# A one-core attention + MLP kernel: a new written-out order of tasks, with the first q and k ahead of w_tok and the casting loads behind the selector and masks

## The chip, the cores and the metric

The kernel runs on one core of a Trainium2 chip. The metric is the device time of one execution in microseconds (us), the median of three runs. The engines are named as the profile names them: PE (TensorE), DVE (VectorE), ACT (ScalarE), POOL (GpSimd) and SP (SyncE, which here only starts transfers). ACT and POOL start transfers too.

## What is computed

Four batches (B = 4) of 768 tokens, 8 heads of 64, so 512 channels. First attention with a window of 128 tokens and 4 sink tokens, then a residual MLP that mixes tokens and channels:

```python
scores = scale * np.matmul(q, k.transpose(0, 1, 3, 2))
keep = is_sink | in_window            # rel in [0, 128), or one of the first 4 keys
a = softmax(where(keep, scores, -1e9))
x = matmul(a, v)                      # heads side by side: (4, 768, 512)

a1  = alpha1 * x + beta1
tok = np.einsum('ts,bsd->btd', w_tok, a1)          # w_tok is 768 x 768
u   = x + lam * tok
a2  = alpha2 * u + beta2
ch  = np.maximum(a2 @ w_ch1, 0.0) @ w_ch2          # 512 -> 2048 -> 512
out = u + lam * ch
```

All inputs and the output are float32 in memory; the matmuls take float16 operands and sum in float32.

## The kernel before

**Stages.** The work is cut per batch. For batch 0: load q, k and v, cast to float16, transpose q and k on PE (`trans`, lines 482 to 535), scores S = k q (`scores`, `scores_by_pair`), exp on ACT, mask, P V (`pv`, lines 707 to 785) with the sums of the softmax from a column of ones, normalisation on DVE (lines 748 and 749). Then `tok` (lines 845 to 873): 36 matmuls of 128x128 by 128x512 with the transposed w_tok, then the transposes of u (`uTp`), `mlp1` (lines 926 to 947: 512 channels to 2048, ReLU), and `mlp2` (for batch 0) or seven products in Strassen's manner (`prod`, for batches 1 to 3). While batch b is in its MLP, the attention of batch b+1 is laid between its matmuls. The start, up to the first `tok` matmul of batch 0, has no earlier batch to be laid beside.

**Tiles.** A q or k tile holds two heads ("hp", a pair, 0 to 3) of all 768 tokens; t = 0 is q, t = 1 is k. For batch 0 the pair 0 is loaded by SP as float32 (`nat0_0_0`, `nat0_0_1`, line 402) and cast on DVE (line 157). The pairs 1 to 3 are loaded by POOL's queue, which casts in flight (`CASTING`, line 322, and line 395); these six transfers are called the casting loads here. v comes in twelve pieces of 128 KB (`load_v0`, line 429), w_tok in six rows of 384 KB (`load_wtok`, line 440), each then cast (`cast_wtok`, lines 819 or 821) and transposed on PE (line 814). w_ch1 comes in four casting transfers of POOL's queue, w1[0] to w1[3] (`load_w1`, line 453), which `mlp1` needs by quarters of its 16 columns fi: fi 0 to 3 need w1[0], 4 to 7 w1[1], 8 to 11 w1[2], 12 to 15 w1[3].

**The selector, masks and identity** are made on POOL: `make_iden` (lines 330 and 331), `make_masks` (five instructions, lines 338 to 348), `make_bm` (the block mask, lines 359 and 363), `make_sel` (lines 370 and 374). `make_bias` (line 353, DVE) turns the masks into a bias that PE adds to the scores.

**The order is written out by hand.** Every step is a task, registered by `add` with a running number. `emit` (lines 54 to 74) walks a table `ORDER` of task numbers and issues each task on the engine that `ENGINES` gives to it by its number (0 ACT, 1 DVE, 2 PE, 3 POOL, 4 SP). Each engine then takes its own instructions strictly in that order. `HOMES` gives every buffer its place: two buffers of one kind and one home share memory, so the later one waits for the readers of the earlier. `IDLES` lists matmuls on zeros ahead of a task, as (task, home of the PSUM bank, how many): they fill PE's waiting time (line 148).

Fixed costs, due times and dependencies in the `add` calls served a planner; at run time only the order, the engines, the homes and the data decide.

**Tasks that the change and the prediction speak of** (number: what, line, engine in the kernel before):

- 6 and 7: loads of q and k of pair 0 (402, SP); 26: first row of w_tok (440, SP); 9, 8, 15, 12, 14, 13: casting loads of k1, q1, k3, q2, q3, k2 (395, POOL)
- 45 and 48: casts of q0 and k0 (157, DVE); 46 and 49: their transposes (512, PE); 47 and 50: copies of these from PSUM (155, ACT)
- 51 and 52: transposes of q1 (509, PE) and their copy (157, DVE); 61 and 62: the same for k3
- 90, 91: scores of pair 0, first key block, and its exp (686, 691); 109, 110: scores of key block 4 for four heads, and their exp (622, 644)
- 63, 64, 65, 66: casts of v pieces; 72 to 89: the six rows of w_tok (cast, transpose, copy); 81 and 82: cast and transpose of row block 3, ahead of `tok`
- 39: product of alpha1 and lam (1169); 43 and 44: transpose of alpha2 and beta2 and its copy
- 115, 118, 121, 124, 127, 130: halves of the float16 input of `tok` (758, POOL); 32 to 35: w1[0] to w1[3]
- 213: the first `tok` matmuls; 295: the first `mlp1` column that needs w1[3]
- 179, 178, 197: the loads `wst_w2_0`, `lam_b` and `wst_w2_12` (449 and 1240, SP); 36: a small transfer on SP that waits for w1[1], and holds back all that stands behind it on SP
- 653, 660: scores of batch 2, key blocks 0 and 1 (622); 656 and 654: the two exps of block 0 (644)

Of the kernel before, what the change touches and what calls it, by code (L numbers as in the profile page):

```python
# [77 lines left out]
def kernel(  # L78
# [119 lines left out]
    for r in range(NR):  # L198
# [18 lines left out]
        26, 6, 9, 7, 10, 5, 11, 8, 18, 15, 72, 19, 1, 12, 3, 0, 4, 2, 22, 14, 73, 74, 45,  # L217
        48, 46, 17, 39, 49, 47, 53, 13, 40, 50, 41, 90, 95, 43, 91, 51, 54, 103, 52, 16, 44,
        61, 104, 42, 96, 109, 100, 62, 107, 110, 63, 55, 28, 108, 92, 56, 101, 21, 68, 65,
        59, 93, 20, 69, 97, 102, 111, 94, 24, 98, 57, 60, 30, 112, 105, 23, 58, 99, 113,  # L220
        128, 106, 114, 116, 25, 131, 135, 78, 115, 64, 27, 138, 31, 32, 117, 132, 29, 129,
        136, 33, 122, 66, 125, 34, 123, 137, 119, 139, 126, 35, 79, 70, 120, 140, 124, 84,
        71, 80, 133, 130, 141, 67, 146, 85, 134, 121, 147, 144, 75, 118, 158, 86, 154, 148,
        159, 145, 142, 87, 149, 150, 155, 160, 143, 76, 88, 151, 156, 81, 77, 166, 152, 162,
        167, 89, 127, 82, 163, 213, 83, 168, 209, 164, 165, 214, 210, 153, 217, 179, 211,
        178, 157, 197, 229, 36, 212, 215, 218, 185, 216, 226, 230, 219, 176, 161, 177, 220,
        169, 223, 222, 232, 225, 224, 221, 227, 237, 233, 279, 238, 234, 228, 273, 280, 182,
        171, 204, 257, 274, 175, 277, 258, 200, 231, 259, 278, 246, 260, 295, 199, 384, 241,
        248, 188, 186, 291, 296, 247, 172, 243, 289, 174, 181, 242, 293, 292, 187, 170, 290,
        267, 37, 294, 271, 358, 268, 198, 285, 349, 272, 381, 301, 286, 366, 351, 303, 302,  # L230
        189, 297, 378, 173, 304, 281, 180, 352, 203, 249, 190, 282, 298, 379, 250, 287, 380,
        192, 353, 385, 288, 206, 283, 386, 369, 375, 367, 265, 284, 368, 202, 370, 266, 363,
        376, 371, 253, 377, 201, 299, 254, 372, 364, 183, 382, 191, 300, 373, 615, 365, 275,
        374, 383, 357, 261, 276, 408, 262, 387, 263, 184, 409, 205, 195, 239, 411, 264, 410,
        395, 269, 396, 240, 397, 270, 196, 388, 614, 621, 235, 412, 400, 194, 244, 398, 236,
        401, 255, 617, 251, 245, 256, 389, 390, 399, 252, 311, 359, 207, 193, 391, 424, 616,
        335, 425, 393, 341, 426, 392, 336, 648, 427, 634, 413, 394, 312, 636, 414, 428, 419,
        404, 420, 415, 360, 405, 313, 429, 208, 422, 337, 416, 361, 441, 421, 622, 402, 314,
        423, 442, 626, 403, 305, 638, 315, 406, 430, 640, 316, 435, 431, 306, 641, 355, 436,
        443, 619, 437, 338, 649, 618, 438, 362, 317, 432, 637, 407, 307, 433, 345, 444, 339,  # L240
        439, 635, 318, 445, 450, 434, 639, 644, 319, 451, 628, 452, 620, 440, 308, 645, 340,
        453, 417, 446, 323, 447, 418, 320, 309, 448, 324, 321, 658, 322, 329, 449, 642, 659,
        454, 325, 625, 643, 330, 646, 347, 455, 326, 623, 343, 647, 464, 344, 456, 465, 348,
        466, 460, 457, 467, 650, 327, 458, 331, 461, 629, 459, 472, 462, 632, 463, 653, 356,
        651, 656, 627, 332, 38, 654, 480, 333, 342, 624, 652, 473, 310, 476, 468, 471, 470,
        469, 481, 474, 488, 885, 477, 475, 482, 492, 655, 490, 493, 350, 483, 478, 514, 491,
        516, 489, 657, 479, 515, 660, 517, 630, 882, 665, 518, 663, 354, 328, 666, 502, 880,
        661, 664, 498, 879, 519, 508, 499, 346, 503, 678, 662, 512, 509, 679, 504, 513, 487,
        484, 671, 485, 676, 486, 506, 677, 877, 548, 505, 672, 680, 507, 526, 549, 546, 527,
        631, 334, 522, 674, 681, 528, 547, 907, 523, 534, 903, 529, 633, 682, 675, 878, 542,  # L250
        683, 535, 890, 689, 543, 550, 685, 684, 690, 510, 551, 494, 511, 673, 667, 544, 495,
        668, 891, 496, 686, 545, 901, 687, 669, 497, 693, 888, 688, 883, 530, 694, 670, 700,
        531, 524, 897, 701, 698, 500, 691, 525, 696, 699, 552, 501, 697, 704, 553, 558, 695,
        705, 904, 692, 562, 559, 706, 909, 887, 707, 563, 564, 898, 708, 702, 566, 565, 910,
        715, 703, 567, 532, 716, 889, 713, 533, 709, 714, 896, 520, 710, 556, 717, 521, 538,
        557, 537, 540, 539, 536, 560, 541, 899, 718, 921, 572, 922, 881, 711, 574, 884, 573,
        576, 712, 561, 719, 902, 577, 575, 555, 727, 720, 569, 908, 721, 580, 728, 578, 722,
        581, 729, 554, 723, 905, 730, 568, 739, 724, 579, 725, 592, 570, 911, 726, 582, 740,
        593, 588, 912, 583, 595, 584, 571, 906, 743, 589, 731, 585, 900, 590, 732, 605, 744,
        587, 733, 596, 606, 734, 607, 611, 594, 597, 602, 745, 612, 586, 613, 599, 895, 603,  # L260
        591, 757, 765, 600, 758, 601, 759, 766, 741, 771, 760, 742, 916, 772, 751, 917, 746,
        773, 752, 913, 761, 919, 774, 886, 767, 918, 604, 762, 763, 598, 768, 777, 764, 779,
        920, 923, 780, 914, 755, 915, 778, 608, 756, 926, 930, 735, 609, 931, 924, 927, 781,
        736, 925, 775, 782, 737, 928, 753, 929, 893, 738, 934, 754, 892, 769, 935, 932, 610,
        941, 770, 819, 776, 942, 894, 939, 820, 821, 940, 937, 936, 823, 749, 822, 945, 748,
        824, 938, 747, 827, 933, 948, 950, 750, 952, 943, 951, 825, 953, 787, 828, 944, 807,
        788, 797, 826, 808, 949, 946, 829, 798, 801, 954, 830, 791, 802, 956, 947, 792, 783,
        955, 957, 963, 961, 784, 789, 958, 962, 811, 790, 964, 959, 785, 812, 965, 805, 786,
        795, 806, 960, 967, 796, 799, 793, 968, 966, 970, 972, 794, 813, 971, 969, 815, 973,
        814, 809, 800, 816, 803, 810, 974, 978, 804, 976, 979, 837, 975, 977, 835, 838, 980,  # L270
        841, 836, 839, 842, 818, 843, 840, 845, 981, 832, 982, 846, 817, 986, 844, 831, 990,
        987, 983, 988, 847, 991, 984, 851, 833, 992, 1002, 993, 834, 848, 855, 852, 985,
        849, 1003, 859, 856, 1004, 989, 1006, 850, 860, 1005, 853, 998, 1007, 1008, 868,
        999, 857, 1009, 997, 865, 995, 858, 862, 996, 869, 866, 1000, 874, 994, 854, 1001,
        1016, 863, 875, 1040, 1017, 1038, 1041, 1032, 1039, 871, 1020, 872, 1028, 1021,
        1011, 1024, 1029, 1013, 1018, 1033, 1012, 1025, 1034, 1019, 1036, 1010, 1035, 1042,
        1037, 1076, 1043, 1070, 1077, 870, 1074, 1071, 1054, 1075, 1022, 1055, 1060, 1023,
        1048, 1061, 1058, 1049, 1066, 1059, 1014, 1044, 1015, 1067, 1072, 1045, 1056, 1073,
        1026, 1057, 1078, 1068, 1079, 1064, 1069, 1046, 1027, 1050, 1063, 1047, 1052, 1082,
        1053, 1051, 1084, 1083, 1062, 1065, 1030, 1085, 1080, 1101, 1031, 1081, 1091, 1102,  # L280
        1107, 1092, 1097, 1093, 1103, 864, 1108, 1105, 867, 1098, 1111, 1106, 1104, 1113,
        1112, 1089, 1114, 1115, 1086, 1116, 1090, 861, 1094, 1087, 1117, 1099, 1109, 1100,
        1121, 1095, 1110, 1125, 1118, 1122, 1124, 1134, 1126, 1123, 1128, 1135, 1127, 1119,
        1136, 1088, 1140, 1120, 873, 876, 1131, 1129, 1141, 1096, 1137, 1142, 1132, 1130,
        1133, 1138, 1139,
    )
    ENGINES = (
        "3313134433443333444444444444444433334441111201201202120212021213030121211201211210200200"
        "2020201202011202020202020213213213213213213202002020202020213121312131213121312131404444"
        "4044413314433334411114413334444042213221321021020121021021321202020020211212021212020212"  # L290
        "1212020202120212120212020202120202020212122221022221422221022221422221022221013111111131"
# [18 lines left out]
        "1202002102135312330203"  # L310
    )
    IDLES = (
        (73, 0, 65), (46, 0, 12), (49, 1, 1), (90, 3, 10), (61, 3, 2), (109, 3, 3), (92, 3,
        1), (166, 1, 4), (162, 0, 1),
    )
    W1_SINCE = 20000.0
# [1011 lines left out]
```

## Time and profile before

| what | value |
|---|---|
| median of three runs | 256.99 us (256.12 to 257.42) |
| the profiled execution's own time | 255.43 us |
| its span (first to last instruction) | 253.2 us |
| TensorE clock granted | 1.00 |
| busy in the span: PE, DVE, ACT, POOL | 245.4, 190.7, 133.3, 102.2 us |
| busy from 32 us to 249 us: PE | 216.94 of 217.00 us |
| first `tok` matmul | 31.96 us |
| last DVE instruction | ends at 249.4 us |

The median belongs to three other executions than the profiled one, which was 1.56 us shorter. Between the span and the profiled execution's own time lie 2.2 us outside the instructions.

How to read the rows of the profile: a row of a timeline has the start in us from the span's start, the duration in us, the engine, the line, the operation, the tiles written and read with their shapes, how many such instructions are merged (x), and in brackets how long the engine had been idle before, and what ended that wait. A row of the chain of waits has the start, the duration, and the engine or transfer that the end of the program hung on at that time. A row of a table by stretches has the busy time of each engine in that stretch.

### The profile page before, as it was taken

The numbers are of one execution on the slowest core, as the hardware profiler recorded it, in microseconds if no ns is written. First come the engines' busy times: TensorE is split into PE (matmuls) and PEld (weight loads), VectorE is DVE, ScalarE is ACT, GpSimd is POOL, SyncE is SP. The second block draws the span as 40 slices with busy tenths as digits, with TensorE's granted clock in tenths as the row PEclk, the third lists the DMA queues.
The fourth block names the chain that finished last, engine by engine and source line by source line (L and its number), as shares of the span: only waits on it lengthen the run. The fifth ranks groups of instructions, "written<-read, shape, count | busy, mean of one in ns | idle before, by whom it ended". The sixth has DMA issues, their size and how long they took to land.

```text
span 253.2 us, 5499 instructions
## 1 busy us (share of the span) xinstructions
PE 245.4 (97%) x2167; PEld 159.8 (63%) x2167; DVE 190.7 (75%) x402; ACT 133.3 (53%) x219; POOL 102.2 (40%) x124
## 2 busy tenths in 40 slices
PE   8699999999999999999999999999999999999993
PEld 7555646676545544566687686567677676667882
DVE  5588987877788874978879986577778983228892
ACT  2499925879976034787932535566660235543000
POOL 8317854895247417525682040065562220000010
PEclk9999999999999999999999999999999999999999
DMA  6999999999979998997485674420000140100317
GB/s 170 207 240 292 229 276 311 330 362 285 221 130 250 247 194 158 192 244 168 107 176 117 114 151 124 132 66 0 3 0 3 38 83 7 41 0 3 122 70 268
DMA packets 86129, 38.79 MB, mean 153 GB/s; under 512 B 73540, under 2 KB 80460, under 8 KB 86104
## 3 DMA queue, kind: packets, MB, share of 16 engines
q1 hardware_dynamic: 66576, 28.06, 46.9%
q10 hardware_dynamic: 15784, 7.11, 11.9%
q0 software_dynamic: 3744, 3.28, 8.3%
q8 instruction: 17, 0.28, 0.5%
q14 instruction: 8, 0.07, 0.1%
HBM read 29.91 MB, written 6.29 MB: 143 GB/s over the span
## 4 chain that ended last, share of the span: by engine, by line
PE 94%; DMA 3%; DVE 0%; SPq 0%; issue 0%
PE h L934 33%; PE P L1051 22%; PE tok L854 12%; PE ch L1119 8%; PE pv L723 5%; PE S L622 4%; DMA nat<-in_k_dram 3%; PE S L617 2%; PE tp L512 1%; PE pv L716 1%; PE tp L509 1%; PE wT L814 1%; PE sk L554 1%; PE idle L148 1%; PE uTp L895 1%; PE pv L609 1%
## 5 line engine op out<-in xcount | busy, mean ns | idle before, releaser
L934 PE MATMUL h<-uT,w1f 128*128 128x384 f16 x512 | 89.6, 327 | 0.0
L934 PEld LDWEIGHTS <-w1f 128*128 128x128 f16 x512 | 48.2, 98 | 31.0 <-issue 1.7
L940 ACT ACTIVATE hT<-h 128x384 f16<-128x384 f32 x77 | 37.0, 491 | 38.0 <-PE h L934 37.9
L1051 PEld LDWEIGHTS <-hT 128*128 128x128 f16 x408 | 39.4, 98 | 6.8 <-issue 0.2
L942 DVE TENSOR_SCALAR hT<-h 128x384 f16<-128x384 f32 x51 | 27.8, 555 | 20.3 <-PE h L934 19.6
L644 ACT ACTIVATE E<-S 128x1024 f16<-128x1024 f32 (+1 forms) x39 | 38.1, 1002 | 8.1 <-PE S L622 6.6
L767 POOL TENSOR_TENSOR tm<-x,la_b 128x512 f32<-128x512 f32 x18 | 24.3, 1350 | 25.2 <-DVE x L749 13.4
L854 PE MATMUL tok<-xh,wtokT 128*128 128x512 f16 x144 | 33.0, 379 | 0.0
L1064 DVE TENSOR_TENSOR x<-x,P 128x256 f32<-128x256 f32 x45 | 18.3, 419 | 11.3 <-PE P L1051 10.2
L1051 PE MATMUL P<-w2f,hT 128*128 128x256 f16 x216 | 26.5, 273 | 0.0
L854 PEld LDWEIGHTS <-wtokT 128*128 128x128 f16 x144 | 13.9, 98 | 15.0
L1119 PE MATMUL ch<-w2f,hT 128*128 128x512 f16 x96 | 23.2, 380 | 0.0
L1051 PE MATMUL P<-w2s,hT 128*128 128x256 f16 x192 | 23.1, 273 | 0.0
L1087 POOL TENSOR_TENSOR x<-x,pt 128x256 f32<-128x256 f32 x4 | 3.4, 855 | 47.5 <-DVE pt L1082 47.5
L155 ACT CAST u<-x 128x512 f16<-128x512 f32 x15 | 9.2, 615 | 24.9 <-DVE x L861 24.3
L749 DVE TENSOR_TENSOR x<-pv,rec 128x256 f32<-128x256 f32 x48 | 20.4, 425 | 1.7
L155 ACT CAST n<-nat 128x768 f16<-128x768 f32 x21 | 16.9, 828 | 7.4 <-DVE x L1130 6.3
L723 PEld LDWEIGHTS <-E 128*128 128x128 f16 x328 | 14.8, 97 | 5.0 <-issue 1.3
L861 DVE TENSOR_TENSOR x<-x,tok 128x512 f32<-128x512 f32 x24 | 16.0, 683 | 2.4 <-PE tok L854 2.3
L723 PE MATMUL pv<-vfs,E 128*128 128x65 f16 x328 | 17.6, 194 | 0.0
L584 POOL TENSOR_SCALAR_AFFINE_SELECT E<-E 128x512 f16<-128x512 f16 x12 | 7.5, 646 | 21.1 <-ACT E L644 21.1
L748 DVE RECIPROCAL rec<-pv 128x4 f32<-128x4 f32 x48 | 8.6, 179 | 7.7 <-PE pv L723 7.1
(134 smaller groups left out, 339.9 us busy)
## 6 DMA issues: line engine op xcount, KB each, us to landing
wst_w<-in_moe_w_ch_dram SPq DMA_DIRECT2D x8, 512.0 KB, 8.3
nat<-in_q_dram SPq DMA_DIRECT2D x10, 384.0 KB, 4.1
vnat<-in_v_dram SPq DMA_DIRECT2D x14, 256.0 KB, 5.4
nat<-in_k_dram SPq DMA_DIRECT2D x8, 384.0 KB, 6.6
out_dram<-x SPq DMA_DIRECT2D x11, 256.0 KB, 3.1
out_dram<-x ACTq DMA_DIRECT2D x10, 256.0 KB, 3.8
wtn<-in_moe_w_tok_dram SPq DMA_DIRECT2D x6, 384.0 KB, 4.5
w1f<-in_moe_w_ch_dram POOLq DMA_DIRECT2D x4, 512.0 KB, 14.0
```

Of the source, the lines that this page charges most:

```text
L155: nc.scalar.copy(o, i)
L644: nc.scalar.activation(eT.t, pS.t[:, :, 0 : n * w].rearrange("p e (i w) -> p e i w", i=n), AF.Exp, scale=scale)
L723: nc.tensor.matmul(po.t[:, hl, :], eT.t[:, e_, off + i, c : c + P], vf[j][:, h, :], start=(r < 2 and n == 0), stop=(n == len(parts) - 1 an ...
L749: nc.vector.tensor_mul(bx.t[:, 4 * G : 4 * G + 4, :], po.t[:, :, 0:D], rec.t.to_broadcast([P, 4, D]))
L767: engine[e].tensor_mul(bt.t, bx.t.rearrange("p h d -> p (h d)"), la1_b)
L854: nc.tensor.matmul(pt.t, wtokT[:, si, ti * P : (ti + 1) * P], hs[si].t, start=(si == 0), stop=(si == NR - 1))
L934: nc.tensor.matmul(ph.t, w1f[:, c, fi * P : (fi + 1) * P], bu.t[:, c, chk * NTOK : (chk + 1) * NTOK], start=(c == 0), stop=(c == NC - 1))
L940: nc.scalar.activation(bh.t[:, fi, :], ph.t, AF.Relu)
L942: nc.vector.tensor_scalar_max(bh.t[:, fi, :], ph.t, 0.0)
L1051: nc.tensor.matmul(pc.t, hh[:, nt * P : (nt + 1) * P], w(fi), start=(first and n_ == 0), stop=(n_ == HF - 1), skip_group_check=True)
L1064: nc.vector.tensor_add(row(bx)[:, cols], row(bx)[:, cols], pc.t)
L1119: nc.tensor.matmul(pc.t, bh.t[:, fi, nt * P : (nt + 1) * P], w2f[:, fi, :], start=(fi == 0), stop=(fi == NF - 1))
```

## The change

Only five tables are exchanged: `ORDER`, `ENGINES`, `HOMES`, `IDLES` and with them the homes of buffers. No task is added or removed, and no instruction has another shape. 41 tasks change their engine, and most entries of `ORDER` up to the first `tok` are new; behind it the order changes by short swaps.

```diff
     ORDER = (
-        26, 6, 9, 7, 10, 5, 11, 8, 18, 15, 72, 19, 1, 12, 3, 0, 4, 2, 22, 14, 73, 74, 45,
-        48, 46, 17, 39, 49, 47, 53, 13, 40, 50, 41, 90, 95, 43, 91, 51, 54, 103, 52, 16, 44,
...
+        6, 7, 0, 26, 1, 10, 5, 9, 11, 45, 18, 8, 2, 19, 48, 3, 22, 46, 15, 4, 49, 12, 50,
+        17, 14, 47, 13, 16, 90, 103, 39, 41, 91, 43, 104, 53, 72, 95, 54, 28, 63, 96, 51,
...
     IDLES = (
-        (73, 0, 65), (46, 0, 12), (49, 1, 1), (90, 3, 10), (61, 3, 2), (109, 3, 3), (92, 3,
-        1), (166, 1, 4), (162, 0, 1),
+        (46, 0, 67), (90, 1, 25), (109, 3, 2), (166, 1, 4), (162, 0, 1),
     )
```

The beginning of each engine's own sequence, read out of the tables:

| engine | before | after |
|---|---|---|
| SP | w_tok row 0, q0, k0, then v | q0, k0, w_tok row 0, then v (unchanged) |
| POOL | k1 load, sel, q1 load, k3 load, masks, q2 load, block mask, identity, q3 load, k2 load, cast 63, cast 65, half 115, w1[0..3], five more halves | identity, masks, sel, k1 load, q1 load, block mask, k3, q2, q3 and k2 loads, product 39, cast 65, half 115, cast 64, halves 130, 118, 127, w1[0..2], half 124, w1[3], half 121 |
| DVE | cast 72 of w_tok row 0, 4, bias, casts 45 and 48, 39, 40, 41, copy 52 of q1 | casts 45 and (behind the bias) 48, 4, copies 50 and 47, 41, cast 72, v cast 63, 42, copy 74, 100 |
| PE | 65 idle, transposes of w_tok row 0, 12 idle, 46, 1 idle, 49, k1, 10 idle, 90 | 67 idle, 46, 49, 25 idle, 90, scores of key block 2, 43, k1 (53), 95, q1 (51), w_tok row 0 (73), 109 |
| ACT | copies 74, 47, 50, exp 91 | exp 91, exp 104, copy 54 of k1, exp 96, copy 52 of q1, exp 110 |

Engine changes before the first `tok`: from ACT to DVE the copies 47, 50, 74 and 86, the v cast 66, the w_tok cast 84 and the small copy 44; from DVE to ACT the copies 52, 62 and 80 and the w_tok casts 75 and 78; from DVE to POOL the product 39; from POOL to DVE the v cast 63; from ACT to POOL the v cast 64. Behind it: some ReLU halves of batch 0 to 3 between ACT and DVE, casts of w_ch2 (194 and 195 to POOL, 183 to DVE), one sum for Strassen (349 to POOL), one cast of k for batch 1 (372 from ACT to POOL), and two loads of batch 1 (171, 177) from ACT's queue to SP's, behind task 36.

Homes that matter below: `v0_1_1`, a piece of v, had the home 3 of its kind, which `wst_w2_0` takes next; now `v0_1_0` and `v0_1_1` have the homes 0 and 1, and the homes 3 and 2 of `wst_w2_0` and `wst_w2_12` have no earlier user. The six casting loads no longer take the place of a buffer that is still to be read, but for q3 (task 14), which takes that of k0.

In the middle, PE's sequence in batch 2's scores was 653, sinks, a part of `ch`, two row blocks of `tok`, five `mlp1` columns, 660; it is now 653, sinks, the same part of `ch`, 660, and then three row blocks of `tok`.

## The prediction

> **What bounds the kernel now.** I read the page's busy times first, then the chain of waits, then the busy time by stretches, and last the timeline of the start.
>
> ```profile
> PE 245.4 (97%) x2167; PEld 159.8 (63%) x2167; DVE 190.7 (75%) x402; ACT 133.3 (53%) x219; POOL 102.2 (40%) x124
> ...
> 1.72 7.97 DMA nat<-in_k_dram
> 9.71 0.57 DVE n L157
> 10.33 0.51 PE tp L512 x6
> ...
> 32.12 6.47 PE tok L854 x30
> ...
> 248.97 0.42 DVE x L1064
> ...
> 12.20:32.00 19.80, 19.74 (x273) 11.08 (x272) 16.88 (x44) 18.93 (x32) 11.67 (x16) 1.00 1.11 253
> 32.00:249.00 217.00, 216.94 (x1778) 140.89 (x1775) 166.40 (x333) 110.67 (x183) 82.99 (x88) 1.00 0.63 141
> ```
>
> The lines from k0's transfer (1.72) to 248.97 are the chain: the end hangs on k0's transfer up to 9.7 us, then on PE. The last two are stretches (PE, weight loads, DVE, ACT, POOL, clock, DMA share, GB/s). From 32 us on PE is busy for 216.94 of 217.00 us at clock 1.00. No swap of the other engines' work can shorten that stretch; it can only open gaps in it. The time to be won lies in the start, where `tok` begins at 31.96, and there ACT is full too: 18.93 of 19.80 us, against DVE's 16.88. So I ask when ACT's row of exps starts, how long it becomes, and what `tok` waits for last.
>
> **Part 1, q0 and k0 ahead of w_tok.** In the trace the first transfer of SP (w_tok row 0) lands 3.2 us after its issue at 0.81, the second (q0) 4.1 us after 1.27: at 4.0 and 5.3. The third (k0) takes 7.97 us. By place in the queue q0 will land at about 4.0 and k0 at 5.3 instead of 9.7. Then 67 idle matmuls hold PE to 1.06 + 67 x 0.079 = 6.4 (65 took 5.15 us). Two transposes (0.34 apart) end at 7.1; the copies 50 and 47 now follow one another on DVE (956 ns for such a copy; starts 0.88 apart) to 9.0; score to exp took 0.33 (11.89 to 12.22). The first exp starts at 9.3 instead of 12.2, **2.9 us earlier**. The 25 idle matmuls (1.7 us, at 0.067 each) end at 8.8, inside this wait.
>
> **Part 2, casting loads behind selector and masks.** This takes most of it back.
>
> ```profile
> 12.37 0.53 PE L509 MATMUL tp<-iden,n 128*64 128x128 f16 x12
> 12.94 0.96 DVE L157 COPY qkT<-tp 128x768 f16<-128x768 f16 x1 [0.72 <-PE tp L509]
> 15.21 1.94 ACT L644 ACTIVATE E<-S 128x1024 f16<-128x1024 f32 x2 [0.62 <-PE S L622]
> DMA to landing us min/median/max: 6.6/8.2/8.9
> ```
>
> The first three lines are the timeline: q1's transposes, their copy, and the first exp over 1024 columns, task 110, which needs pairs 0 and 1. The fourth is the casting loads' time from issue to landing. POOL's masks take 1.40 us (4.41 to 5.81), the selector 0.68 (2.31 to 2.99), the block mask 0.5. The masks cannot start before their memsets (1.59), so k1 goes out at 3.8 instead of 1.3, q1 at 4.6 instead of 2.9, k3 at 5.8 instead of 3.7; q2 at 6.5 for 5.8, q3 at 7.3 for 7.5, and k2 at 8.0 instead of 10.6, since it no longer waits for k0's cast. But the loads landed by one another's pace, not by issue: k1 at 9.4, q1 at 11.25, k3 at 12.6, q2 at 14.0, 1.4 to 1.9 apart. With q0, k0 and w_tok row 0 gone by about 6 us, I take for k1 a little less than k2's 6.6, which still had q3 ahead of it until 15.4: landed at 9.8, then q1 at 11.2, k3 at 12.6. The other end is the old 8.1 us: 11.9 for k1 and 13.3 for q1.
>
> A rule of the Trainium skill speaks against the lower end. "SBUF — State Buffer", section "SBUF: two separate sides", says that GpSimd cannot write the descriptors of its transfers while VectorE runs an operation that uses both ports, such as a float32 copy from SBUF to SBUF. The casts 45 and 48 (560 ns each) will now stand at 4 to 6 us, amid the POOL issues, and the bias (219 and 350 ns) with them. By the rule this is up to 2 x 0.56 + 0.57 = 1.7 us of delay for q1, and all that this part leaves of the gain is gone. By the rows it is little: the issue at 7.47, with the bias beside it, took 713 ns, that at 5.77 with DVE idle 722; k3's at 3.69, beside w_tok's cast (953 ns), took 721, though it had the longest landing, 8.9 against 8.3. I go by the rows (0.6 at most), and keep the rule's price in the range.
>
> In the trace q1 landed at 11.25, but its transposes stood behind the first scores until 12.37. There k0's chain was the last to arrive; now q1's load is. From its transposes to the exp it took 2.84 us. Of these go 0.16 (the copy is on ACT, 800 ns for 956) and 0.34, in which PE was at k3's transposes and idle matmuls after the copy's end (13.90 to 14.24); w_tok row 0's transposes, now in that place, fit beside the copy. 11.2 + 0.1 + 2.4 = 13.7 instead of 15.2. **1.5 us earlier.** The other 1.4 of Part 1 wait for this load.
>
> **Part 3, what ACT has to do from there to the last w_tok cast (81).** Away go two v casts (622 and 827 ns), a w_tok cast (0.83 from start to start) and the copy of row block 4 (807): 3.1 us. Added are the copy of k3 (800), two w_tok casts (0.83 each) and the copy of row block 2 (807): 3.3. ACT is full here, so **0.2 us later**. DVE's sum stays within its 2.9 us of slack: it gives and takes about the same. POOL gets the product 39 (1.2) and a v cast (0.61) and loses one; it was idle for 8.1 of the 19.8 us, so nothing, unless the halves ahead of `tok` come late: these have 0.6 us to spare (the last one needed ends at 31.38).
>
> **Part 4, the end of the start.** The last cast ends at 31.15 and `tok` starts at 31.96, because a group of eight `pv` matmuls (31.37) and one of transposes stand between. Now the exps that `pv` needs come first, and two transposes (0.34 each) are left: **0.3 us earlier**. Sum of the start: -1.5 + 0.2 - 0.3 = **-1.6 us**; `tok` at 30.4.
>
> **Part 5, w_ch1's loads, later on POOL.** w1[0..2] stand behind v cast 64 and three more halves (0.61 + 3 x 0.69 = 2.7 us), w1[3] behind a fourth. With half 115 about 1.4 earlier, they go out 1.3 later, w1[3] 2.0 later. The trace has 8.6, 12.2, 15.9 and 20.9 us to landing: w1[3] at 44.5, and PE's first column on it starts at 44.80. This is the tightest cover of the kernel. Beside it `wst_w2_0`, `lam_b` and `wst_w2_12` no longer wait for a v buffer until 26.64 and go out at about 22, so they fall into the rest of w_tok's loading and leave the engines earlier to w1; and SP's later loads are held by task 36 until w1[1] is there. The same bytes in all have to pass, so I price it between 0 and, if w1[3] lands as much later as it is issued (46.5) while PE asks for it 1.6 earlier (43.2), 3.3 us. I take 0: these loads are 1.25 MB, more than the 0.4 MB that two microseconds move at 200 GB/s (207 in the stretch from 27 to 30 us).
>
> **Part 6, in the middle.**
>
> ```profile
> 97.75 0.61 PE L622 MATMUL S<-qkT 64*128 64x256 f16 x8
> 98.29 0.40 PE L554 MATMUL sk<-qkT,ks 128*32 128x512 f16 x4
> 98.40 1.02 ACT L644 ACTIVATE E<-S 128x1024 f16<-128x1024 f32 x1 [3.64 <-PE S L622]
> 99.32 1.02 ACT L644 ACTIVATE E<-S 128x1024 f16<-128x1024 f32 x1
> ```
>
> Task 660 writes the two score banks that 653 filled, and the one it writes first is read last (task 654 stands behind 656). Both exps are done at 100.34; sinks and the part of `ch` end at 99.66. Task 660, put right there, waits **0.7 us**, and behind it on PE stand three row blocks of `tok` that could run. In the trace two of these and five `mlp1` columns lay between. Nothing covers it: ACT had been idle before (3.64 us). The other end, 0, would need exps that start before PE's eight matmuls are through.
>
> All other swaps behind `tok` (ReLU between ACT at 491 and DVE at 555 ns, w_ch2 casts to POOL at 1390 where DVE took 760, k's cast 372 to POOL) I cost at nothing: PE's four small banks and ACT's 53% hide them; without cover each costs its own 0.5 to 1.4 us. 171 and 177 on SP wait behind 36, for w1[1]; their casts come some 8 us later. The tail (249 to 253.2, 4.2 us of it without PE) keeps its order: 0.
>
> **Sum**: -1.6 + 0 + 0.7 = **-0.9 us**. Against the profiled 255.43 this is 254.5. The runs shown lie higher (median 256.99), so on that footing **256.1 us**; 0.5%, or 1.3 us, is about what a measurement of this kernel can tell from no change.
>
> **Rivals.**
>
> - **The start comes through whole (faster).** q1 lands before 11, ACT keeps its pace, w1[3] is early: -2.3 to -1.4 in all, about **255.2**. For it: k0's chain is 2.9 us earlier, and 1.4 of this is left over; the DMA share of 1.11 says that engines, not issues, set the landings. Against it: PE has no slack for Part 6.
> - **w1[3] late (slower).** One place, PE at column 15 of `mlp1`, batch 0. It decides once w1[3] lands after 43.2; from there each us of landing is a us, since PE keeps its order. -1.6 + 3.3 + 0.7 = +2.4: **259.4**; half that delay gives 257.7. For it: 0.3 us of margin in the trace. Against it: the early w_ch2 loads.
> - **The casting loads late, by the rule or by 8.1 us of latency.** q1 at 13.3: the start is -1.6 + 2.1 = +0.5, the whole +1.2; with the rule's delay on top up to +2.9. About **258.6**. For it: three of the six had over 8.2 us; against it, that the row shows landings in step, not latency.
> - **VectorE and GpSimd don't meet less.** POOL gains about 1.2 us of work before `tok`, and a v cast of 768 columns on DVE took 945 ns beside POOL's halves where a q cast of the same shape took 560 alone. If the two further v casts on DVE (63, 66) meet POOL, 0.4 each: the sum goes to about -0.1, **256.9**.
>
> **Chances.** The sum with its own range, 255.2 to 256.9: 0.45, of which 0.17 lies beyond 0.5% (under 255.7). Start whole: 0.24, all beyond. w1[3] late: 0.16, and casting loads late: 0.10, of which 0.02 stay within 0.5%. Meeting no less: 0.05. So faster 0.41, same 0.28 + 0.02 + 0.05 = 0.35, slower 0.24. The range leaves about one in ten on either side: 254.6 to 258.9 holds the sum, most of the whole start and half of the slower cases.
>
> **What would show it.** First exp (691) at 9.3; q1's transposes (509, the second group) at 11.3 and the first exp over 1024 columns near 13.7; `tok` near 30.4; column 15 of `mlp1` without a gap at 43.2; a gap of PE of 0.7 before batch 2's second score block near 99; then the same 217 us. I am wrong if casting loads land over 9 us after issue, if ACT shows gaps over 0.5 us from 14 to 30, or if PE has gaps behind `tok` of over 1 us.

## The result, and the profile after

| | median of runs | profiled execution | its span |
|---|---|---|---|
| before | 255.67 us (22 runs, 254.22 to 261.47) | 255.43 | 253.2 |
| changed | 256.86 us (22 runs, 255.88 to 257.89) | 256.29 | 254.2 |

The ratio is 1.0046, with a 95% interval of 1.0025 to 1.0068: the change makes the kernel **slower by 0.46%**, 1.2 us. I had forecast 0.9 us faster (256.1 beside a median of 256.99 from three runs). 256.86 lies in the range given, but the sign is wrong. All ratios are taken over fast runs alone and are not the quotients of the medians beside them (for e12 below the ratio is 0.9948, the quotient 0.9963), and of three profiled executions that lie well above the median of their kernel (those of e2 and e2b below, and the first of e10) only the starts, waits and tails named are read.

The changed kernel's page, and its busy time by stretches (PE, weight loads, DVE, ACT, POOL, clock, DMA share, GB/s):

```profile
PE 245.8 (97%) x2167; PEld 160.2 (63%) x2167; DVE 194.0 (76%) x400; ACT 132.5 (52%) x219; POOL 108.4 (43%) x126
```

```profile
12.20:32.00 19.80, 19.37 (x255) 10.60 (x254) 17.12 (x45) 18.11 (x30) 12.82 (x18) 1.00 1.11 273
32.00:249.00 217.00, 215.53 (x1764) 140.22 (x1763) 166.99 (x327) 110.47 (x184) 86.50 (x87) 1.00 0.61 137
249.00:254.00 5.00, 0.65 (x6) 0.33 (x4) 0.65 (x2) 0.00 (x0) 0.00 (x0) 0.91 0.74 256
```

Before, PE worked 216.94 of the 217 us in the middle row; now it lacks 1.47 us there and still has 0.65 us of matmuls behind 249. POOL is busy 6.2 us longer and DVE 3.3 us longer for the same program. Three rows of the chain of waits after the change, at the start of `tok` and at the end:

```profile
30.48 3.67 PE tok L853 x17
...
235.89 13.77 PE P L1050 x126
...
249.68 0.42 DVE x L1063
```

By the chain `tok` begins at 30.48 instead of 32.12, 1.64 us earlier, as forecast. (The timeline, which the figures for `tok` below use, has the first matmul at 30.31 instead of 31.96.) Yet PE's last matmul ends at 249.65 instead of 248.94. Somewhere between the two 2.35 us are lost. The view of PE's waits (what it waited for, sum, times, longest), from 31 to 250 us, names three; for the kernel before, the same view is empty behind the start of `tok`:

```profile
PE S L621 <- ACT E L643: 0.7, 1, 0.7
PE vsp_None L572 <- DVE hT L941: 0.4, 1, 0.4
PE h L933 <- DVE x L860: 0.3, 1, 0.3
```

Counted from the start of one matmul to the next, less its usual step, these are 0.80 us (at 97.5), 0.53 (60.1) and 0.45 (40.6). Smaller ones add 0.25 at 182.7 and 0.12 at 208.4, and the remaining 0.2 is spread over many small ones. From PE's last matmul to the end it is 4.52 us instead of 4.30. So: -1.64 + 2.35 + 0.22 = +0.93 us, the difference of the two spans (254.17 and 253.24).

### The profile page after: what moved, and what is told of

The parts are those of the page before. It is cut to its first block, busy times and chain, and to the rows that moved or that the text cites. A ratio compares the mean times of both kernels' runs of the same rounds, so it can differ in the third digit from the quotient of the medians.

```text
span 254.2 us, 5511 instructions
## 1 busy us (share of the span) xinstructions
PE 245.8 (97%) x2167; PEld 160.2 (63%) x2167; DVE 194.0 (76%) x400; ACT 132.5 (52%) x219; POOL 108.4 (43%) x126
## 4 chain that ended last, share of the span: by engine, by line
PE 87%; ACT 3%; DVE 3%; DMA 3%; POOL 1%; issue 1%; POOLq 0%; ACTq 0%; DVEq 0%
PE h L933 31%; PE P L1050 22%; PE tok L853 12%; PE ch L1118 8%; PE pv L722 4%; PE S L621 4%; DMA n<-in_q_dram 3%; PE S L616 1%; PE tp L511 1%; ACT E L643 1%; ACT wt L818 1%; PE tp L508 1%; PE pv L715 1%; PE wT L813 1%; DVE w2f L835 1%
## 5 line engine op out<-in xcount | busy, mean ns | idle before, releaser
L1050 PEld LDWEIGHTS <-hT 128*128 128x128 f16 x408 | 39.5, 98 | 7.2 <-DVE hT L993 0.6
L155 ACT CAST u<-x 128x512 f16<-128x512 f32 x17 | 10.3, 616 | 28.8 <-DVE x L860 27.3
L1086 POOL TENSOR_TENSOR x<-x,pt 128x256 f32<-128x256 f32 x4 | 4.0, 997 | 46.0 <-DVE pt L1081 46.0
L155 ACT CAST n<-nat 128x768 f16<-128x768 f32 x20 | 16.2, 830 | 8.1 <-DVE xh L769 6.7
L583 POOL TENSOR_SCALAR_AFFINE_SELECT E<-E 128x512 f16<-128x512 f16 x12 | 8.4, 723 | 17.5 <-ACT E L643 17.5
L1118 PEld LDWEIGHTS <-hT 128*128 128x128 f16 x96 | 8.8, 98 | 9.3 <-issue 0.2
```

The lines of the kernel that those rows point to most:

```text
L155: nc.scalar.copy(o, i)
L1050: nc.tensor.matmul(pc.t, hh[:, nt * P : (nt + 1) * P], w(fi), start=(first and n_ == 0), stop=(n_ == HF - 1), skip_group_check=True)
L1118: nc.tensor.matmul(pc.t, bh.t[:, fi, nt * P : (nt + 1) * P], w2f[:, fi, :], start=(fi == 0), stop=(fi == NF - 1))
```

## Experiments

Each ratio is to the kernel before, timed beside it on the same chip. The main ones first; the rest stand with their runs.

| kernel | median / before | ratio, 95% interval | `tok` starts at |
|---|---|---|---|
| e1: start of the change, rest of before | 255.17 / 255.51 | 0.9981 [0.9963, 0.9998] | 30.60 |
| e2b: before to 51 us, rest of the change | 256.84 / 255.14 | 1.0075 [1.0051, 1.0099] | |
| e3: change, 660 back | 256.04 / 255.51 | 1.0030 [1.0012, 1.0047] | 30.32 |
| e6: change, four moves | 255.27 / 255.51 | 0.9999 [0.9978, 1.0019] | 30.09 |
| e4: change, cast 202 apart | 256.48 / 255.14 | 1.0045 [1.0028, 1.0062] | 30.56 |
| **e12: before, GpSimd's new order alone** | 254.21 / 255.16 | **0.9948 [0.9924, 0.9971]** | 30.49 |

### Start or rest?

```diff
 e1: ORDER, ENGINES and HOMES of the changed kernel for its first 191 tasks,
-    of the changed kernel from there on
+    of the kernel before from there on
```

> The changed kernel's first 191 tasks (with their engines, homes and idle matmuls, up to the first row blocks of tok), and all the rest as in the kernel before. Theory A (the rest of the change opens the waits): tok starts near 30.5, PE has no wait of over 0.15 us behind it that the kernel before lacks, and the time is 1.6 us below the kernel before (ratio 0.994). Theory B (an early tok alone opens them, since VectorE and GpSimd are no earlier): new waits of 1 to 1.6 us in all behind tok, and the time within 0.5 us of the kernel before.

Measured: `tok` at 30.60, but 0.35 and 0.43 us of waits at 39.4 and 39.9 and 0.22 at 45.6, which the kernel before lacks: 1.0 us of the gain is given back at once, and 0.5 us is left. B is right for the region near 40 us and for the time; none of the later waits is there, so A is right for the rest.

The opposite join first failed:

> The kernel before up to its task 171 (start, tok not yet begun), and all the rest as in the changed kernel. Theory A: tok near 32, the same waits of PE as in the changed kernel (0.80 at the second score block of batch 2, 0.53 at the w_ch2 cast, 0.45 at the fourth column, 0.25 and 0.12 later), and the time 2.0 to 2.7 us above the kernel before (ratio 1.008 to 1.010). Theory B: only the wait at the second score block and the 0.25 remain, about 1.1 us above (1.004).

The junction at task 171 lies inside the start and spoiled it: the median of six runs is 261.16 us (ratio 1.0192 [1.0141, 1.0242]), `tok` at 37.4 in the profiled execution. It tells nothing of the rest. The next one joins behind the start.

```diff
 e2b: the kernel before for its first 268 tasks (to about 51 us),
-     the kernel before from there on
+     the changed kernel from there on
```

> As the run before of the same aim, but joined where the two orders can be joined without disturbing the start: the kernel before up to its task 268 (about 51 us: start, tok and the first fifteen columns of mlp1), and the rest as in the changed kernel. Theory A (the rest of the change costs by itself): tok at 32, no new wait near 40, then 0.80 us at task 660, up to 0.53 at the cast 183, 0.25 at the sum 955 and 0.12 later, the tail 0.27 longer: 1.5 to 2.0 us above the kernel before (ratio 1.006 to 1.008). Theory B (the early start makes them): 0.9 us or less above (1.0035).

1.7 us above the kernel before by the medians, 1.9 by the ratio: A. Without any change in the start, the rest of the change loses this time by itself, with waits of 0.80 at task 660, 0.64 at the cast 183, 0.25 and 0.12, and a tail of 4.55. Near 40 us there is no new wait, so those at 40.6 belong to the start of the change.

### The waits one by one

```diff
 e3, PE's sequence:
-332, 660, 472, 480, 665, 476, 488, 492, 490, 514, 516, 518
+332, 472, 480, 665, 476, 488, 492, 490, 514, 516, 660, 518
```

> The changed kernel with task 660 alone moved back on PE behind the mlp1 columns, to where the kernel before has it. Theory A: the wait of 0.80 us goes and nothing takes its place, 0.8 us below the changed kernel (about 256.0 where before has 255.7, ratio 1.0015). Theory B: something else is late right behind it and takes 0.3 us or more of it back (ratio 1.003 or more).

The changed kernel at this wait, and ahead of it the exps that hold the score banks (timeline):

```profile
97.53 1.02 ACT L643 ACTIVATE E<-S 128x1024 f16<-128x1024 f32 x1
98.60 0.61 PE L621 MATMUL S<-qkT 64*128 64x256 f16 x8 [0.73 <-ACT E L643]
```

With 660 moved back this wait is gone, and 0.25 us comes back at 99.5, where 665 (`pv`) now waits. By the ratios 0.4 us is won (1.0046 to 1.0030): the figure of B.

The second wait needs two traces. The changed kernel near 59 us (start, duration):

```profile
58.49 1.27 POOL L835 TENSOR_TENSOR w2f<-wst_w,lam_b 128x512 f16<-128x512 f32 x1
58.77 1.53 DVE L835 TENSOR_TENSOR w2f<-wst_w,lam_b 128x512 f16<-128x512 f32 x1
...
60.22 0.54 DVE L941 TENSOR_SCALAR hT<-h 128x384 f16<-128x384 f32 x1
...
60.82 0.39 PE L572 MATMUL vsp_None<-vfs,sel 128*128 128x512 f16 x1 [0.36 <-DVE hT L941]
```

and the run with 660 back, whose program is the same up to here:

```profile
58.79 0.68 DVE L835 TENSOR_TENSOR w2f<-wst_w,lam_b 128x512 f16<-128x512 f32 x1
58.83 1.77 POOL L835 TENSOR_TENSOR w2f<-wst_w,lam_b 128x512 f16<-128x512 f32 x1
...
59.39 0.55 DVE L941 TENSOR_SCALAR hT<-h 128x384 f16<-128x384 f32 x1
...
60.31 0.38 PE L572 MATMUL vsp_None<-vfs,sel 128*128 128x512 f16 x1
```

The same two instructions, 183 on DVE and 202 on POOL, take 1.53 and 1.27 us when POOL starts first, and 0.68 and 1.77 when DVE starts first, here by 0.04 us. The later one stands until the earlier is nearly through. "SBUF — State Buffer", section "SBUF: two separate sides", of the Trainium skill says it so, of a VectorE operation with two SBUF inputs beside a GpSimd one that reads SBUF: whichever of the two starts first has the shared ports for its whole instruction. The rule would let 183 end at 59.76 + 0.68 = 60.44 in the first trace and 202 at 59.47 + 1.27 = 60.74 in the second; the traces have 60.30 and 60.60, both 0.14 earlier. So which of the two starts first decides whether the ReLU behind 183, and PE behind that, is late. Of the five traces with this order POOL is first in four (the changed kernel, e2, e2b, e9; PE waits 0.51 to 0.64 us) and DVE in one.

```diff
 e4, POOL's sequence:
-372, 201, 357, 202, 410, 401
+372, 201, 357, 410, 202, 401
```

> The changed kernel with POOL's w_ch2 cast 202 alone moved on POOL, behind the masks 410, so that VectorE's cast 183 has no POOL cast beside it and stays ahead of ReLU 262. Theory A (the meeting costs, not the place in the order): 183 takes 0.68 us instead of 1.53, PE's wait of 0.53 at 60.1 us goes, 0.3 to 0.5 us below the changed kernel (ratio about 1.003). Rival (the cast is simply too long ahead of the ReLU): 183 still takes over 1.2 us or the wait stays above 0.3.

183 takes 0.68 us, the ReLU starts at 59.62 and the wait is gone: A in the trace. In the time nothing is to be seen (1.0045 against 1.0046), though the interval doesn't exclude the 1.003 of A. In the trace 0.15 us comes back at 70.2, and `tok` had started 0.25 later than in the changed kernel, before the edit acts.

```diff
 e6, four tasks, on the engines that the change gave them:
 PE:   660 as in e3
 DVE: -183, 262    +262, 183
 DVE: -227, 169    +169, 227
 DVE: -962, 955    +955, 962
```

> The changed kernel with four tasks moved in the order, each on the engine that the change gave it: 660 behind the columns, the w_ch2 cast 183 on VectorE behind ReLU 262, the beta step 169 ahead of 227, the sum 955 ahead of 962. Theory A: the waits at 40.6, 60.1, 97.5 and 182.7 go, 2.0 us below the changed kernel and 0.8 below the kernel before (ratio 0.997). Theory B: 1.0 us below the changed kernel at most (ratio 1.001 or more).

The waits at 60.1, 97.5 and 182.7 are gone, that at 40.6 shrinks to 0.31, 0.25 stands at 99.2. Together the four places are worth 1.2 us by the ratios (1.0046 to 0.9999): the mechanism of A, at 0.6 of its size. The wait at 182.7 is a meeting of the two engines again: the sum 955 took 0.69 us before, and in the changed kernel, begun while POOL was at a mask (to 181.91),

```profile
181.36 1.09 DVE L769 TENSOR_TENSOR xh<-tm,lb_b 128x512 f16<-128x512 f32 x1
```

with a column of `mlp1` 0.25 us later behind it.

### What in the start is worth what

```diff
 e7 (start of the change, rest of before), POOL's sequence:
-identity, masks, sel, k1, q1, block mask, k3, q2, q3, k2
+identity, k1, sel, q1, k3, masks, q2, block mask, q3, k2
```

> The run with the changed kernel's start and the rest of before, with the first four casting loads (k1, q1, k3, q2) put ahead of masks and block mask again; only the identity and the selector stay among them. Predicted by the row of landings in step: k1 is issued some 2 us earlier but q1 lands at most 0.8 us earlier (10.3 or later), and tok starts within 0.4 us of 30.6. Rival (the loads behind the masks cost the start by their issue): q1 lands over 1.5 us earlier and tok starts before 29.8.

q1 went out at 3.04 instead of 4.28 and landed at 10.68 instead of 10.56: as predicted, its landing doesn't follow its issue. Yet the ratio rises from 0.9981 to 1.0060 [1.0034, 1.0086], 2.0 us (1.3 by the medians), and `tok` starts at 34.0 in the profiled execution (which is itself 1.9 us above the median). Neither theory had what the chain of waits shows:

```profile
3.98 9.89 DMA v<-in_v_dram
13.90 0.04 DVE vfs L157
...
16.49 0.27 PE vsp L572
...
17.81 0.60 ACT E L690
```

It is a piece of **v**, on SP, that is late: landed at 13.9. In the kernel before it landed at 13.5, in e1 at 8.4, in the changed kernel at 9.5. Its cast 63, which the change moved to VectorE, now holds up the alpha and beta rows queued behind it, and through them PE.

```diff
 e8 (start of the change, rest of before), SP's sequence:
-q0, k0, w_tok row 0, v
+w_tok row 0, q0, k0, v
```

> The run with the changed kernel's start and the rest of before, with w_tok's row 0 ahead of q0 and k0 on SP again. Predicted from Part 1: k0 lands some 3 us later, the first exp at 12.0 instead of 9.5, and tok about 1.5 us later (32.0); PE's waits near 40 us shrink from 1.0 to under 0.3, so the time is only 0.5 us above and equals the kernel before (ratio 1.000). Rival (only the order of the casts, engines and homes counts): tok within 0.5 us of 30.6 and ratio 0.998.

First exp at 10.50 instead of 10.03, `tok` at 31.08 instead of 30.60, ratio 0.9998 [0.9977, 1.0020]. SP's order is worth 0.5 us in the traces, not 1.5; by the ratios 0.4, with intervals that overlap. The larger part of the earlier exp must come from elsewhere, so I put one part of the change into the kernel before, alone:

```diff
 e12 (kernel before, nothing else changed), POOL's sequence:
-k1, sel, q1, k3, masks, q2, block mask, identity, q3, k2
+identity, masks, sel, k1, q1, block mask, k3, q2, q3, k2
```

> The kernel before with one part of the change: GpSimd's order identity, masks, selector, k1, q1, block mask, k3, q2, q3, k2; SP, the other engines and the rest as before. Theory (casting loads that stand back leave k0 and v the DMA engines): k0 lands near 6.5 instead of 9.7, the first exp near 10.5 instead of 12.2, v's first half is cast before 12, and tok starts 0.5 us or more earlier. Rival (they only come later): q1 lands after 12, tok at 32 or later, ratio 1.000 or more.

The outcome is as forecast: v's piece landed at 8.23 instead of 13.47, the first exp started at 10.22 instead of 12.22, `tok` at 30.49 instead of 31.96, and **the kernel is 0.5% faster than before** (1.3 us by the ratio, 0.9 by the medians). Its page and a stretch:

```profile
PE 245.8 (98%) x2167; PEld 160.5 (64%) x2167; DVE 191.8 (76%) x402; ACT 133.2 (53%) x219; POOL 102.5 (41%) x124
```

```profile
32.00:249.00 217.00, 215.47 (x1769) 140.46 (x1767) 167.03 (x331) 109.84 (x182) 81.61 (x85) 1.00 0.61 141
```

The 215.47 are no wait: PE's last matmul ends at 247.47, 1.47 us before that of the kernel before, and the view of waits is empty from 31 to 250 us. DVE and POOL are busy 1.1 and 0.3 us longer than before, not 3.3 and 6.2.

That the loads' standing back makes this gain is shown only in part, since the new order also makes the identity first, which PE's transposes read. The kernel before (two rows), the same start in e2b (one) and e12 (one):

```profile
7.57 0.50 PE L814 MATMUL wT<-iden,wt 128*128 128x128 f16 x6 [1.37 <-POOL iden L331]
9.71 0.56 DVE L157 CAST n<-nat 128x768 f16<-128x768 f32 x1 [1.05 <-DMA nat<-in_k_dram]
```

```profile
8.13 1.12 DVE L157 CAST n<-nat 128x768 f16<-128x768 f32 x2 [0.51 <-PE wT L813]
```

```profile
7.06 1.06 DVE L157 CAST n<-nat 128x768 f16<-128x768 f32 x2 [0.84 <-PE wT L813]
```

Before, w_tok's first transposes wait for the identity, and q0's cast (8.11) for them; in e12 both casts are done at 8.12. And k0, late in the kernel before, is not so in e2b with the same order: there the first exp starts at 11.30. So about 1 us of the earlier exp is the identity's, and the rest varies between executions. In the new start e7 keeps the identity first, and there the loads alone cost what is said above. How the 1.5 us of `tok` in e12 divide between identity, k0 and v no run shows.

With this order, SP's can be tried alone as well:

> The kernel before with GpSimd's new order (casting loads behind selector and masks) and, on top, q0 and k0 ahead of w_tok's row 0 on SP; nothing else. Theory (the order on SP adds the 0.5 us that it was worth in the changed start): first exp 9.7 instead of 10.2, tok 30.0 to 30.3, ratio 0.993. Rival (VectorE's and ScalarE's orders still begin with w_tok's row 0, so they wait for it): first exp 10.2 or later, ratio 0.995 or more.

Ratio 0.9989 [0.9967, 1.0011], first exp at 11.67, `tok` at 31.41: the rival. VectorE's queue begins with the cast of w_tok's row 0, which SP now brings later, and k0's cast stands behind it.

### The waits near 40 us

The new order alone has `tok` at 30.49 without them; the whole new start has them. Five runs asked why.

```diff
 e10, e10_again: e1 with ENGINES of 225: -DVE +ACT
 e14: e1, DVE:   -77, 159, 167, 163, 149     +149, 77, 159, 167, 163
 e15: e6 with the same move of 149
 e16: e1, PE:    -213, 209, 217, 214, 210    +213, 209, 214, 210, 217
          DVE:   -157, 218, 211, 215         +211, 157, 215, 218
          DVE:   -221, 169, 225              +169, 225, 221
          ACT:   -219, 212, 216              +212, 216, 219
```

> The run with the changed kernel's start and the rest of before, with the copy 225 (one of the four that fill batch 0's uT) on ScalarE instead of VectorE. Theory (VectorE's row of work behind the early tok makes the two waits near 40 us, 0.35 + 0.43): 225 ends near 39.6 on ScalarE, the sums 227 and 233 run 0.45 earlier, both waits go, 0.7 us below that run (ratio to before 0.9955). Rival (tok's own results or w_ch1 are late there): one of the waits stays and the ratio is 0.9975 or more.

> The run with copy 225 on ScalarE once more, for its trace alone, since the profiled execution of the first was disturbed. Theory (VectorE's row of work): no wait of over 0.15 us near 40 us. Rival: 0.35 or 0.43 stays.

Ratio 0.9981 [0.9962, 1.0001], the same as e1. In the second trace the wait for the copy is gone, and 0.40 at 39.4 and 0.50 at 45.0 stand instead, the latter for ScalarE's ReLU: the work was only handed on.

> The run with the changed kernel's start and the rest of before, with one step of VectorE put back: the beta step 149 of row block 0 ahead of the w_tok copy 77, as in the kernel before, instead of behind the last norms. Theory C (the new start put this step where it meets GpSimd's last halves, 1.65 us instead of 0.74, and that lateness makes PE's waits near 40): 149 takes under 0.9 us, the sums 227 and 233 come 0.7 to 0.9 us earlier, the waits of 0.35 and 0.43 go, ratio to before 0.995. Rival (the waits belong to any tok at 30.5): they stay above 0.5 in sum, ratio 0.998.

> The changed kernel with the four moves in the order (660, 183, 169, 955) and the beta step 149 ahead of 77. Theory C: the 0.3 us at 39.7 goes as well, 0.3 to 0.5 us below the run with four moves (ratio 0.998). Rival: no difference to that run (ratio 1.000).

C falls. Earlier, the step 149 still meets GpSimd's halves (1.20 us), and `tok` starts later (31.42 in e14, 31.74 in e15); in e14 both waits stay, 0.35 and 0.43, in e15 the one of 0.31. Ratios 1.0025 [1.0005, 1.0045] and 1.0025 [1.0007, 1.0042]: worse than without the move.

> The run with the changed kernel's start and the rest of before, with the last row of that start put back to the kernel before: PE finishes tok's row blocks 1 and 0 before it begins 2, VectorE takes the sums 211, 215, 218 in that order with the beta steps between, 169 and 225 ahead of 221, ScalarE the casts 212, 216, 219. Theory D (this order makes VectorE idle until the first sum and late from there, which is PE's waits near 40): the first sum starts 2.9 us after tok instead of 3.2, the waits sum to under 0.4 instead of 0.78, ratio to before 0.996. Rival (they hang on the beta step 149, which takes 1.65 us beside GpSimd's halves): the waits stay above 0.6, ratio 0.998.

The first sum of `tok` started 2.79 us after `tok`, as D had it, and the wait came back in one piece (PE's waits):

```profile
PE h L933 <- DVE uT L879: 0.7, 1, 0.7
```

0.9 us counted from start to start, ratio 0.9992 [0.9971, 1.0013]: D falls as well. What remains, argued and not tested, is that VectorE is late as a whole there: in e12 the step 149 was done at 27.9 in 0.74 us and ten instructions of VectorE stood behind the first sum, in e16 it ends at 32.6 and eleven do. Which of the start's moves on VectorE makes this isn't settled.

### The tail, and two loads on SP

```diff
 e9: ENGINES of 171 and 177: -SP +ACT
 e11: e6 with the same, and 225 on ACT
```

> The changed kernel with the two loads 171 and 177 back on ScalarE's queue instead of SP's. Theory (two more transfers on SP make the last stores' issues 0.9 to 1.0 us instead of 0.33): the last three stores of SP take 0.33 again, from PE's last matmul to the end 4.3 us instead of 4.55, 0.25 us below the changed kernel (ratio about 1.0035). Rival (the issue times have another cause): they stay at 0.9 or more and the time as in the changed kernel (1.0045).

> The changed kernel with all repairs: the four moves in the order (660, 183, 169, 955), the copy 225 on ScalarE, the loads 171 and 177 on ScalarE's queue. Theory: the 0.3 us at 39.7 and 0.25 us of the tail go, 0.5 us below the run with four moves (ratio 0.998). Rival: the 0.25 at 99.2 and the longer row of meetings of VectorE and GpSimd keep it at the kernel before (ratio 1.000).

The tail stays (0.98 us for the last store, 4.53 us), so the number of transfers on SP, 111 again as before the change, isn't the cause. The time rises to ratios of 1.0154 [1.0103, 1.0205] and 1.0113 [1.0072, 1.0155], from six and seven runs, which neither theory had. In the changed order the load 177 waits until a load of q has landed that SP issues only at 36.54, behind task 36 and so behind w_ch1; on ScalarE's queue everything behind it waits with it (timeline of e9):

```profile
43.27 0.87 ACT L939 ACTIVATE hT<-h 128x384 f16<-128x384 f32 x2 [4.26 <-DMA nat<-in_q_dram]
...
43.81 0.97 PE L933 MATMUL h<-uT,w1f 128*128 128x384 f16 x5 [1.38 <-ACT hT L939]
```

Their move to SP is thus needed by the rest of the change. The tail's 0.2 to 0.3 us stays open: it is there in every kernel that has the changed order at the end (4.52 to 4.73 us against 4.25 to 4.31), though the stores' order on SP is the same.

## Why the prediction was wrong

- **Start, -1.6 us: right in size.** q0 and k0 landed at 3.94 and 5.06 (4.0 and 5.3 forecast), the first exp started at 9.52 (9.3), q1 landed at 11.06 (11.2), the first exp over 1024 columns started at 13.04 (13.7), `tok` at 30.31 (30.4). The path through q1's load is the one in the chain of the changed kernel.
- **Its division: wrong, so the sum is in part luck.** Part 1 gave the gain to SP's order and Part 2 named the casting loads as what "takes most of it back". It is the other way round: GpSimd's order alone has nearly the whole start (30.49), SP's order is worth 0.5 us in the new start (e8) and costs in the old one (e13). I had seen that casting loads land by one another's pace, and not asked who gains when they stand back: a piece of v landed 4 to 5 us earlier. Nor had I asked what waits for the identity.
- **The rule weighed in Part 2** (the Trainium skill, "SBUF — State Buffer", "SBUF: two separate sides"; 1.7 us by its price): beside VectorE's casts of q0 and k0 (3.96 to 5.66 us) the issues of k1 and q1 took 0.90 and 0.72 us (0.90 and 0.75 before), and q1 landed 6.8 us after its issue, not later than before (8.3). No effect is seen here; the rows were right.
- **Part 5, w_ch1 later: right at 0,** with a margin that I had not seen: w1[3] was issued 2.5 us later and landed at 40.96 instead of 44.5, and no column waited for it. The rival falls.
- **Part 6, +0.7: right,** 0.73 in the timeline. Moved back, it yields 0.4 us by the ratios, since a later `pv` waits instead.
- **The step that failed: "All other swaps behind `tok` ... I cost at nothing: PE's four small banks and ACT's 53% hide them".** They cost 1.1 us of PE in the profiled execution (0.53 + 0.25 + 0.12 + 0.2), and a further 0.45, at 40.6, comes with the start's new order of VectorE (e1 has waits there, e2b none), for which there was no term either. The 53% are an average over the whole span; a bank is freed by the one instruction that reads it, on an engine that works in order. A cast put ahead of a ReLU, which takes 1.53 us beside GpSimd instead of 0.68, was enough. The price that I named, "without cover each costs its own 0.5 to 1.4 us", was nearer than the 0 that I took, and I had not looked place by place whether the cover was there. Its sign, "gaps behind `tok` of over 1 us", came true with 2.35. (So did the one for the casting loads, k2 with 9.4 us to landing, without harm.)
- **"The tail ... keeps its order: 0": wrong** by 0.22 us, for a cause that stays open.
- **The rival "VectorE and GpSimd don't meet less"** was right in kind among the slower ones, with a chance of 0.05 and a price of 0.8 us taken from the start alone; the meetings that cost PE lie at 60.1 and 182.7. By the two traces, both engines are busy at once for 76.2 us before and 84.0 after; with GpSimd's order alone it is 78.3. By groups of one line, tiles and shape, instructions that kept their engine take some 5 us longer in all on VectorE and 3 on GpSimd, and 3.4 us more work lies on GpSimd.
- **Sum.** From -0.9 to +0.9 in the profiled executions: 1.1 for the swaps behind `tok`, 0.45 for the wait at 40.6, 0.2 for the tail, 0.1 for Part 6. By the ratios the experiments divide the change so: GpSimd's order -1.3 us (e12), the other changes of the start +0.8 (e1 less e12), the rest +1.9 (e2b); their sum of 1.4 stands beside a measured 1.2. By the medians the three are -0.9, +0.6 and +1.7.

## What to carry to other kernels

When an early transfer is moved back, ask which transfers on the other queues land earlier for it; what the moved one loses may be nothing. On an engine without slack, every instruction put ahead of one that frees its banks has to be followed to the bank, at the duration it has beside its neighbour and not at the one it has alone. A gain and its losses that come in one table of orders are best taken apart: here one line of ten tasks on GpSimd carried the whole gain.

## What had not been expected of the hardware

- Casting loads on GpSimd's queue hold back loads of SP's queue without landing sooner themselves: with k1, q1 and k3 issued 1.2 to 1.9 us earlier (e7 against e1), a piece of v lands at 13.9 us instead of 8.4. In the four traces with the early casting loads it lands at 13.5 to 14.7, in the others with the late ones at 8.2 to 10.3.
- An elementwise instruction over two SBUF operands on VectorE and one on GpSimd hardly overlap: 0.68 us becomes 1.53, or 1.27 becomes 1.77, by which started first; a lead of 0.04 us was enough.
- SP's last two stores take 0.9 to 1.0 us each to issue with one order of the program and 0.33 with another, with the same stores in the same order on SP. No run here shows why.
